# A decode block with its backward pass: a third of the score tiles shared with ScalarE, a reordered start-up, and V loads on another queue

## The chip, the cores and the metric

The kernel runs on one core of one Trainium2 chip. The metric is device time in microseconds (us) from the first to the last instruction, of single executions; I quote medians. The engines are called PE (matmul), DVE (vector), ACT (scalar), POOL (GpSimd) and SP (sync); each has its own instruction list, and in the traces here ran it as laid out (in the changed kernel the reciprocal comes 9 score tiles behind the maximum, in the list and in the trace alike).

## The reference, cut to what matters

One token passes an attention layer with 32 heads over a cache of 8192 positions, then a small MLP; the gradients of nearly all inputs are wanted too. What the change touches is the forward attention:

```python
D, Hq, Sk, Dh = 640, 32, 8192, 192
mod = (silu(c) @ w_mod)                        # 640 x 3840, six vectors of 640
h = layernorm(x) * (1 + ca) + sa
q = h @ wq                                     # 640 x 6144
scores = einsum('bhqd,bhkd->bhqk', q, k) * Dh ** -0.5
p = softmax(scores); o = einsum('bhqk,bhkd->bhqd', p, v)
x = x + ga * (o @ wo)
# ... MLP with w3, w4; then the gradients, among them dk and dv of 100 MB each
```

K and V of one head are 3.15 MB each in bf16. They are read once forward and once backward, and dK and dV are written.

## The kernel before

A head's K lies in the on-chip memory (SBUF) as 128 partitions x 64 tiles x 192. Five large buffers (`big`, tag `kv`) hold K, V and, when needed, weights. For a head DVE does 64 fused multiply-and-reduce instructions, one for each tile:

```python
    for h in range(H):
        Kt = big.tile([P, NT, Dh], BF16, tag="kv", name="Kt");  nc.sync.dma_start(out=Kt, in_=Kd[h])      # h > 0
        Vt = big.tile([P, NT, Dh], BF16, tag="kv", name="Vt");  nc.scalar.dma_start(out=Vt, in_=Vd[h])
        # ... wo for a pair of heads
        for t in range(npe, NT):
            nc.vector.tensor_tensor_reduce(out=junk_tile(Dh), in0=Kt[:, t, :], in1=qb, ...,
                                           op0=ALU.mult, op1=ALU.add, accum_out=sT[:, t:t + 1])
        nc.vector.reduce_max(out=mx, in_=sT, axis=AX.X)                # "the maximum"
        # ... PE transpose, DVE max, PE broadcast, ACT scale
        nc.scalar.activation(out=eT, in_=sT, func=ACT.Exp, bias=negb, scale=scale, accum_out=rs)
        nc.tensor.matmul(z_ps, lhsT=ones_f, rhs=rs, start=True, stop=True)
        nc.vector.reciprocal(out=rZb_all[:, h:h + 1], in_=z_ps)        # "the reciprocal"
        for t in range(NT):
            nc.tensor.matmul(o_ps, lhsT=eT_bf[:, t:t + 1], rhs=Vt[:, t, :], ...)
        nc.scalar.activation(out=o_row, in_=o_ps, func=ACT.Copy, scale=rZb_all[0:1, h:h + 1])
        # ... o_row to columns of oT, by PE and ACT
        if h % 2 == 1:
            nc.vector.tensor_copy(out=oT_bf[...], in_=oT[...])         # "the column copy"
            # ... 15 small matmuls with wo
        if h == max(0, H - 3):
            # ... load w3 on SP and w4 on ACT into two of the five large buffers
```

The program is written in dataflow; a compile-time scheduler fixes the order of every engine's list from its own model of durations, and inserts the waits.

## Time and profile before

| | before |
|---|---|
| median of 16 runs | 1883.7 us (1877.7 to 1887.1) |
| first score tile starts | 68.25 us |
| maximum of the last head | 682.80 us |
| from there to the end | 1199 us |
| DVE busy / idle between these two | 592.4 / 22.1 us |

The prediction shows the strips and windows. Two lines more from the page of before: source and destination, issuing queue, count, size, and the median us from issue to landing.

```profile
Kt<-in_A_k_cache_dram SPq DMA_DIRECT2D x32, 3072.0 KB, 13.7
Vt<-in_A_v_cache_dram ACTq DMA_DIRECT2D x32, 3072.0 KB, 14.9
```

And what DVE waited for in 100 to 600 us (total us, times, longest):

```profile
DVE ao_part L478 <- PE ao_ps L475: 5.7, 9, 0.6
DVE gm L452 <- PE mxT_ps L450: 1.1, 3, 0.7
DVE rZb_all L463 <- PE z_ps L462: 1.0, 4, 0.3
```

DVE hardly waits for anything in the steady heads.

### The profile page before, as it was taken

The numbers are of one execution on the slowest core, as the hardware profiler recorded it, in microseconds if no ns is written. First come the engines' busy times: TensorE is split into PE (matmuls) and PEld (weight loads), VectorE is DVE, ScalarE is ACT, GpSimd is POOL, SyncE is SP. The second block draws the span as 40 slices with busy tenths as digits, with TensorE's granted clock in tenths as the row PEclk, the third lists the DMA queues.
The fourth block names the chain that finished last, engine by engine and source line by source line (L and its number), as shares of the span: only waits on it lengthen the run. The fifth ranks groups of instructions, "written<-read, shape, count | busy, mean of one in ns | idle before, by whom it ended". The sixth has DMA issues, their size and how long they took to land.

```text
span 1881.7 us, 25108 instructions
## 1 busy us (share of the span) xinstructions
PE 635.7 (34%) x5307; PEld 523.1 (28%) x5307; DVE 1724.4 (92%) x11076; ACT 876.4 (47%) x2603; POOL 1.7 (0%) x12
## 2 busy tenths in 40 slices
PE   5145443554455452223232232322313223232232
PEld 3134433443344341112131221211212112121120
DVE  2599999999999767999999999999999999999987
ACT  1000000000000013767867777776776777777660
POOL 0000000000000000000000000000000000000000
PEclk9567766676667665556566565655656656565565
DMA  9778888888888741999999999999999999999995
GB/s 385 301 288 351 341 358 334 352 350 340 353 343 359 296 156 44 383 392 409 398 406 390 413 413 390 400 426 394 405 399 398 396 401 419 406 399 409 398 354 212
DMA packets 82263, 675.41 MB, mean 359 GB/s; under 512 B 4662, under 2 KB 50492, under 8 KB 57532
## 3 DMA queue, kind: packets, MB, share of 16 engines
q1 hardware_dynamic: 45656, 345.26, 46.7%
q10 hardware_dynamic: 36452, 328.54, 41.9%
q14 instruction: 114, 0.93, 0.1%
q8 instruction: 41, 0.67, 0.1%
HBM read 447.88 MB, written 225.91 MB: 358 GB/s over the span
## 4 chain that ended last, share of the span: by engine, by line
DVE 58%; DMA 23%; PE 5%; issue 1%; ACT 1%; DVEq 0%; SPq 0%; ACTq 0%
DVE junk L445 20%; DVE junk L644 20%; DMA out_dram<-dKst 13%; DMA Vt_b<-in_A_v_cache_dram 10%; DVE dKst L658 7%; DVE dVst L634 2%; PE dq_ps L668 2%; PE o_ps L466 1%; DVE junk L712 1%; DVE junk L591 1%; DMA Kt<-in_A_k_cache_dram 1%; DVE sT L445 1%; DVE junk L680 1%; DVE dpT L644 1%; PE c_ps L202 1%
## 5 line engine op out<-in xcount | busy, mean ns | idle before, releaser
L644 DVE CUSTOM_DVE_ANT_0 junk<-Vt_b,do_bcast 128x192 bf16<-128x192 bf16 x2048 | 576.0, 351 | 14.1 <-DMA Vt_b<-in_A_v_cache_dram 14.0
L445 DVE CUSTOM_DVE_ANT_0 junk<-Kt,q_bcast 128x192 bf16<-128x192 bf16 x2048 | 578.1, 345 | 8.2 <-DMA Kt<-in_A_k_cache_dram 8.1
L632 ACT ACTIVATE dVst<-do_bcast,pT 128x192 bf16<-128x192 bf16 x1536 | 541.9, 443 | 50.1 <-DVE dhAT L684 43.0
L668 PE MATMUL dq_ps<-Kt_b,dsT_bf 128*1 128x192 bf16 x2048 | 238.5, 294 | 638.2 <-ACT dsT_bf L652 616.1
L668 PEld LDWEIGHTS <-dsT_bf 128*1 128x1 bf16 x2048 | 202.7, 101 | 696.8 <-ACT dsT_bf L652 668.4
L658 DVE TENSOR_SCALAR dKst<-q_bcast,dsT 128x192 bf16<-128x192 bf16 x1376 | 249.4, 262 | 1.8 <-DVE dsT L650 0.3
L656 ACT ACTIVATE dKst<-q_bcast,dsT 128x192 bf16<-128x192 bf16 x672 | 235.5, 440 | 4.0 <-ACT dsT_bf L652 4.0
L466 PE MATMUL o_ps<-Vt,eT_all 128*1 128x192 bf16 x2048 | 227.5, 286 | 0.0
L466 PEld LDWEIGHTS <-eT_all 128*1 128x1 bf16 x2048 | 196.5, 98 | 23.8
L468 ACT ACTIVATE o_row<-o_ps,rZb_all 1x192 f32<-1x192 f32 x32 | 13.2, 412 | 405.3 <-PE o_ps L466 183.5
L644 DVE DVE_READ_ACCUMULATOR2_ANT dpT<- 128x1 f32 x2048 | 163.7, 80 | 0.0
L445 DVE DVE_READ_ACCUMULATOR2_ANT sT<- 128x1 f32 x2048 | 151.9, 74 | 0.0
L634 DVE TENSOR_SCALAR dVst<-do_bcast,pT 128x192 bf16<-128x192 bf16 x512 | 94.4, 260 | 0.0
L652 ACT CAST dsT_bf<-dsT 128x64 bf16<-128x64 f32 x32 | 7.8, 244 | 164.5 <-DVE dsT L650 164.5
L456 ACT ACTIVATE negb<-nb_ps 128x1 f32<-128x1 f32 x32 | 5.5, 171 | 156.7 <-PE nb_ps L454 155.6
L475 PE MATMUL ao_ps<-oT_bf,wof 128*128 128x1 bf16 x240 | 8.6, 165 | 136.9 <-DVE oT_bf L471 136.9
L209 PE MATMUL c2b_tp<-ident_f,doT 128*3 128x128 f32 x16 | 6.0, 374 | 122.8 <-DVE doT L591 122.8
L475 PEld LDWEIGHTS <-wof 128*128 128x128 bf16 x240 | 8.8, 104 | 136.6 <-issue 136.4
L454 PE MATMUL nb_ps<-gm,ones_f 1*128 1x1 f32 x64 | 15.7, 313 | 89.8 <-DVE gm L452 89.8
L680 DVE CUSTOM_DVE_ANT_0 junk<-wqb,dq_b 128x384 bf16<-128x384 bf16 x80 | 43.9, 549 | 0.8 <-ACT dq_b L131 0.8
L591 DVE CUSTOM_DVE_ANT_0 junk<-wob,dao_b 128x640 bf16<-128x640 bf16 x48 | 37.1, 817 | 2.8 <-DMA wob<-in_A_wo_dram 1.8
L209 PEld LDWEIGHTS c2b_tp<-ident_f,doT 128*3 128x3 f32 x16 | 1.3, 81 | 135.3 <-DVE doT L591 135.3
(220 smaller groups left out, 581.8 us busy)
## 6 DMA issues: line engine op xcount, KB each, us to landing
Kt<-in_A_k_cache_dram SPq DMA_DIRECT2D x32, 3072.0 KB, 13.7
Vt<-in_A_v_cache_dram ACTq DMA_DIRECT2D x32, 3072.0 KB, 14.9
Vt_b<-in_A_v_cache_dram SPq DMA_DIRECT2D x32, 3072.0 KB, 17.9
Kt_b<-in_A_k_cache_dram SPq DMA_DIRECT2D x32, 3072.0 KB, 15.4
out_dram<-dVst ACTq DMA_DIRECT2D x32, 3072.0 KB, 18.8
out_dram<-dKst ACTq DMA_DIRECT2D x32, 3072.0 KB, 22.4
wq_sb<-in_A_wq_dram SPq DMA_DIRECT2D x3, 2560.0 KB
wof<-in_A_wo_dram SPq DMA_DIRECT2D x16, 480.0 KB, 11.3
```

The costliest lines, as they stand in the source:

```text
L202: nc.tensor.matmul(ps, lhsT=m, rhs=prodp[:, cc:cc + 1], start=(i == 0), stop=(i == len(pieces) - 1))
L445: nc.vector.tensor_tensor_reduce(out=junk_tile(Dh), in0=Kt[:, t, :], in1=qb, scale=1.0, scalar=0.0, op0=ALU.mult, op1=ALU.add, accum_out=s ...
L466: nc.tensor.matmul(o_ps, lhsT=eT_bf[:, t:t + 1], rhs=Vt[:, t, :], start=(t == 0), stop=(t == NT - 1))
L591: nc.vector.tensor_tensor_reduce(out=junk_tile(D), in0=wob[:, k, :], in1=dao_b, scale=1.0, scalar=0.0, op0=ALU.mult, op1=ALU.add, accum_ou ...
L632: nc.scalar.activation(out=dVst[:, t, :], in_=dob, func=ACT.Copy, scale=pT[:, t:t + 1])
L634: nc.vector.tensor_scalar(out=dVst[:, t, :], in0=dob, scalar1=pT[:, t:t + 1], scalar2=None, op0=ALU.mult)
L644: nc.vector.tensor_tensor_reduce(out=junk_tile(Dh), in0=Vt[:, t, :], in1=dob, scale=1.0, scalar=0.0, op0=ALU.mult, op1=ALU.add, accum_out= ...
L656: nc.scalar.activation(out=dKst[:, t, :], in_=qb, func=ACT.Copy, scale=dsT[:, t:t + 1])
L658: nc.vector.tensor_scalar(out=dKst[:, t, :], in0=qb, scalar1=dsT[:, t:t + 1], scalar2=None, op0=ALU.mult)
L668: nc.tensor.matmul(dq_ps, lhsT=dsT_bf[:, t:t + 1], rhs=Kt[:, t, :], start=(t == 0), stop=(t == NT - 1))
L680: nc.vector.tensor_tensor_reduce(out=junk_tile(W), in0=wqb[:, j, 0:W], in1=dq_b[:, 0:W], scale=1.0, scalar=0.0, op0=ALU.mult, op1=ALU.add, ...
L712: nc.vector.tensor_tensor_reduce(out=junk_tile(WH), in0=wm_sb[:, j, q2 * WH:(q2 + 1) * WH], in1=dmod_b[:, m0 * P + q2 * WH:m0 * P + (q2 + ...
```

## The change

Its intent: give DVE less work per score tile by letting ACT, nearly idle in the forward pass, do a third of the reductions; and start the first head before all weights are there. The diff's core, cuts marked:

```diff
-        Kt0, Vt0 loads; modulation chunks 0 and 1; all three blocks of wq; modulation chunks 2 to 5
+    wmA = mod_load(0, 2 * DC)                      # all on the sync queue, in this order
+    wqA = wq_load(0, [0, WQCH])
+    # K of head 0, K of head 1, V of head 0, rest of the first wq block
+    mod_use(0, 2 * DC, wmA)                        # ... layer norm ...
+    wq_use(0, 0, WQBIG, wqA, "s")
@@ the heads
-            nc.scalar.dma_start(out=Vt, in_=Vd[h])
+            nc.gpsimd.dma_start(out=Vt, in_=Vd[h])
@@ the score tiles
+                if (t % fwd_act_den) < fwd_act_num:          # 1 of 3: 22 of 64
+                    pr = prodq.tile([P, Dh], BF16, tag="prod", name="prod")      # six buffers
+                    nc.vector.tensor_tensor(out=pr, in0=Kt[:, t, :], in1=qb, op=ALU.mult)
+                    nc.scalar.activation(out=pr, in_=pr, func=ACT.Copy, accum_out=sT[:, t:t + 1])
+                else:
                     nc.vector.tensor_tensor_reduce(...)
@@ after a head
+        if h in (5, 12):  # wq blocks 2 and 3: load and use
+        if h == 18:       # modulation columns 10 to 24: load and use
+        if h == 22:       # modulation columns 25 to 29: load and use
# ... rows of c, x, grad_out on the sync queue with three buffers; junk tiles 640 wide instead of 768
```

Three things are changed at once: the start-up with the moved loads, the split of the tiles, and the queue of V.

More of the change, by code (lines that the diff above doesn't have):

```diff
@@ L49 @@
     fwd_pe_groups: int = 0,
+    fwd_act_num: int = 1, fwd_act_den: int = 3,
     bwd_pe: bool = False,
@@ L96 @@
     junkp = ctx.enter_context(tc.tile_pool(name="junkp", bufs=3))
+    prodq = ctx.enter_context(tc.tile_pool(name="prodq", bufs=6))
     psum = ctx.enter_context(tc.tile_pool(name="psum", bufs=2, space=bass.MemoryType.PSUM))
-    JW = max(D, 6 * P, Dh, 768)
+    JW = max(D, Dh, 512)
     def junk_tile(width):
@@ L102, in junk_tile, with big_view @@
         return jt[:, 0:width]
+    def big_view(name, a, b):
+        assert a * b <= NT * Dh
+        t = big.tile([P, NT, Dh], BF16, tag="kv", name=name)
+        flat = t.rearrange("p t d -> p (t d)")
+        return flat[:, 0:a * b].rearrange("p (a b) -> p a b", b=b)
     ident_bf = const.tile([P, P], BF16, name="ident_bf")
@@ L316, in dots_via_pe @@
                 nc.tensor.matmul(out_ps[:, t:t + 1], lhsT=VB[:, tl, :], rhs=col[0:DhB, 1:2], start=False, stop=True)
-    with tc.tile_pool(name="ldrows", bufs=2) as ldrows:
-        cT = load_row_as_col(c_row_d, DC, "cT", nc.sync, ldrows)
-        xT = load_row_as_col(x_row_d, DC, "xT", nc.scalar, ldrows)
-        gT = load_row_as_col(g_row_d, DC, "gT", nc.scalar, ldrows)
+    ldrows = ctx.enter_context(tc.tile_pool(name="ldrows", bufs=3))
+    cT = load_row_as_col(c_row_d, DC, "cT", nc.sync, ldrows)
+    xT = load_row_as_col(x_row_d, DC, "xT", nc.sync, ldrows)
+    gT = load_row_as_col(g_row_d, DC, "gT", nc.sync, ldrows)
     sigT = const.tile([P, DC], FP32, name="sigT")
@@ L338, with mod_load, mod_use @@
     WQCH = 512
-    def big_view(name, a, b):
-        assert a * b <= NT * Dh
-        t = big.tile([P, NT, Dh], BF16, tag="kv", name=name)
-        flat = t.rearrange("p t d -> p (t d)")
-        return flat[:, 0:a * b].rearrange("p (a b) -> p a b", b=b)
+    def mod_load(k, k1):
+        wmt = big_view("wm_sb", DC, (k1 - k) * P)
+        nc.sync.dma_start(out=wmt, in_=wm_d[:, :, k * P:k1 * P])
+        return wmt
+    def mod_use(k, k1, wmt):
+        for m0 in range(k, k1, WMC):
+            m1 = min(k1, m0 + WMC)
+            col_times_wT_to_col(modT[:, m0:m1], wmt[:, :, (m0 - k) * P:(m1 - k) * P], scT_bf, DC, m1 - m0, "mod")
@@ new lines, with wq_load, wq_use @@
+    WQBIG = 2048
+    def wq_load(b0, cuts):
+        wq_sb = big_view("wq_sb", DC, WQBIG)
+        for c0, c1 in zip(cuts[:-1], cuts[1:]):
+            nc.sync.dma_start(out=wq_sb[:, :, c0:c1], in_=wq_d[:, :, b0 + c0:b0 + c1])
+        return wq_sb
+    def wq_use(b0, c0, c1, wq_sb, eng=None):
+        for n0 in range(c0, c1, WQCH):
+            bp = psum.tile([P, WQCH], FP32, tag="bc", name="q_bp")
+            for j in range(DC):
+                nc.tensor.matmul(bp, lhsT=hArep[:, j, :], rhs=wq_sb[:, j, n0:n0 + WQCH],
+                                 start=(j == 0), stop=(j == DC - 1))
+            evac(q_bcast[:, b0 + n0:b0 + n0 + WQCH], bp, eng)
@@ L345 @@
+    wmA = mod_load(0, 2 * DC)
+    wqA = wq_load(0, [0, WQCH])
     Kt0 = big.tile([P, NT, Dh], BF16, tag="kv", name="Kt")
     nc.sync.dma_start(out=Kt0, in_=Kd[0])
+    Kt1 = big.tile([P, NT, Dh], BF16, tag="kv", name="Kt")
+    nc.sync.dma_start(out=Kt1, in_=Kd[1])
     Vt0 = big.tile([P, NT, Dh], BF16, tag="kv", name="Vt")
-    nc.scalar.dma_start(out=Vt0, in_=Vd[0])
-    with tc.tile_pool(name="prow", bufs=2) as prow:
-        def mod_chunk(k):
-            m0, m1 = k * WMC, min(MC, (k + 1) * WMC)
-            wm_sb = prow.tile([P, DC, WMC * P], BF16, tag="wm", name="wm_sb")
-            nc.sync.dma_start(out=wm_sb[:, :, 0:(m1 - m0) * P], in_=wm_d[:, :, m0 * P:m1 * P])
-            col_times_wT_to_col(modT[:, m0:m1], wm_sb, scT_bf, DC, m1 - m0, "mod")
-        mod_chunk(0)
-        mod_chunk(1)
-        saT = modT[:, 0 * DC:1 * DC]
-        caT = modT[:, 1 * DC:2 * DC]
-        layernorm_col(xT, DC, n0T, r0, "ln0")
-        nc.vector.tensor_scalar(out=ca1, in0=caT, scalar1=1.0, scalar2=None, op0=ALU.add)
-        nc.vector.tensor_tensor(out=hAT, in0=n0T, in1=ca1, op=ALU.mult)
-        nc.vector.tensor_tensor(out=hAT, in0=hAT, in1=saT, op=ALU.add)
-        nc.vector.tensor_copy(out=hArep, in_=hAT.unsqueeze(2).to_broadcast([P, DC, P]))
-        WQBIG = (NT * Dh) // DC
-        WQBIG -= WQBIG % WQCH
-        assert WQBIG >= WQCH
-        for b0 in range(0, HD, WQBIG):
-            b1 = min(HD, b0 + WQBIG)
-            wq_sb = big_view("wq_sb", DC, WQBIG)
-            nc.sync.dma_start(out=wq_sb[:, :, 0:b1 - b0], in_=wq_d[:, :, b0:b1])
-            for n0 in range(b0, b1, WQCH):
-                n1 = min(b1, n0 + WQCH)
-                bp = psum.tile([P, WQCH], FP32, tag="bc", name="q_bp")
-                for j in range(DC):
-                    nc.tensor.matmul(bp[:, 0:n1 - n0], lhsT=hArep[:, j, :], rhs=wq_sb[:, j, n0 - b0:n1 - b0],
-                                     start=(j == 0), stop=(j == DC - 1))
-                evac(q_bcast[:, n0:n1], bp[:, 0:n1 - n0])
-        for k in range(2, (MC + WMC - 1) // WMC):
-            mod_chunk(k)
@@ new lines @@
+    nc.sync.dma_start(out=Vt0, in_=Vd[0])
+    nc.sync.dma_start(out=wqA[:, :, WQCH:WQBIG], in_=wq_d[:, :, WQCH:WQBIG])
+    mod_use(0, 2 * DC, wmA)
+    saT = modT[:, 0 * DC:1 * DC]
+    caT = modT[:, 1 * DC:2 * DC]
+    layernorm_col(xT, DC, n0T, r0, "ln0")
+    nc.vector.tensor_scalar(out=ca1, in0=caT, scalar1=1.0, scalar2=None, op0=ALU.add)
+    nc.vector.tensor_tensor(out=hAT, in0=n0T, in1=ca1, op=ALU.mult)
+    nc.vector.tensor_tensor(out=hAT, in0=hAT, in1=saT, op=ALU.add)
+    nc.vector.tensor_copy(out=hArep, in_=hAT.unsqueeze(2).to_broadcast([P, DC, P]))
@@ L422 @@
         else:
-            Kt = big.tile([P, NT, Dh], BF16, tag="kv", name="Kt")
-            nc.sync.dma_start(out=Kt, in_=Kd[h])
+            if h == 1:
+                Kt = Kt1
+            else:
+                Kt = big.tile([P, NT, Dh], BF16, tag="kv", name="Kt")
+                nc.sync.dma_start(out=Kt, in_=Kd[h])
             Vt = big.tile([P, NT, Dh], BF16, tag="kv", name="Vt")
-            nc.scalar.dma_start(out=Vt, in_=Vd[h])
+            nc.gpsimd.dma_start(out=Vt, in_=Vd[h])
         if h % 2 == 0:
@@ L444 @@
             for t in range(npe, NT):
-                nc.vector.tensor_tensor_reduce(out=junk_tile(Dh), in0=Kt[:, t, :], in1=qb, scale=1.0, scalar=0.0,
-                                               op0=ALU.mult, op1=ALU.add, accum_out=sT[:, t:t + 1])
+                if (t % fwd_act_den) < fwd_act_num:
+                    pr = prodq.tile([P, Dh], BF16, tag="prod", name="prod")
+                    nc.vector.tensor_tensor(out=pr, in0=Kt[:, t, :], in1=qb, op=ALU.mult)
+                    nc.scalar.activation(out=pr, in_=pr, func=ACT.Copy, accum_out=sT[:, t:t + 1])
+                else:
+                    nc.vector.tensor_tensor_reduce(out=junk_tile(Dh), in0=Kt[:, t, :], in1=qb, scale=1.0, scalar=0.0,
+                                                   op0=ALU.mult, op1=ALU.add, accum_out=sT[:, t:t + 1])
         mx = small.tile([P, 1], FP32, tag="mx", name="mx")
@@ L479 @@
             nc.vector.tensor_tensor(out=aoutT, in0=aoutT, in1=ao_part, op=ALU.add)
+        if h in (5, 12):
+            wqn = wq_load((1 if h == 5 else 2) * WQBIG, [0, WQBIG])
+            wq_use((1 if h == 5 else 2) * WQBIG, 0, WQBIG, wqn, "s")
+        if h == 18:
+            wmB = mod_load(2 * DC, MC - DC)
+            mod_use(2 * DC, MC - DC, wmB)
+        if h == 22:
+            wmC = mod_load(MC - DC, MC)
+            mod_use(MC - DC, MC, wmC)
         if h == max(0, H - 3):
@@ L544 @@
     dn2T = work.tile([P, DC], FP32, tag="dn2T", name="dn2T")
-    FH = F // 2
-    dn2p = work.tile([P, DC, 2], FP32, tag="dn2p", name="dn2p")
+    NQ = (F + JW - 1) // JW
+    FH = F // NQ
+    assert FH * NQ == F
+    dn2p = work.tile([P, DC, NQ], FP32, tag="dn2p", name="dn2p")
     for j in range(DC):
-        for q2 in range(2):
+        for q2 in range(NQ):
             nc.vector.tensor_tensor_reduce(out=junk_tile(FH), in0=w3_sb[:, j, q2 * FH:(q2 + 1) * FH],
```

## The prediction

> **What bounds the kernel now.** I read the strip of busy tenths first, because the kernel has stages with different limits.
>
> ```profile
> DVE  2599999999999767999999999999999999999987
> ACT  1000000000000013767867777776776777777660
> ...
> DMA  9778888888888741999999999999999999999995
> ```
>
> One column is 47 us. The vector engine (DVE) is full nearly everywhere. In the first two columns it is not: the kernel is loading. Columns 3 to 14 are the forward pass over 32 heads: DVE full, the scalar engine (ACT) almost empty, DMA at 8 tenths. From column 17 on, the backward pass, DMA is full as well. The diff touches start-up and forward pass only, so I cut the time into stages with the view of windows:
>
> ```profile
> core 0: us, PE busy (x) PEld busy (x) DVE busy (x) ACT busy (x) POOL busy (x), PEclk, DMA share, GB/s
> 68.00:683.00 615.00, 281.08 (x2488) 242.07 (x2488) 592.81 (x4244) 41.07 (x187) 0.00 (x0) 0.67 0.82 331
> 683.00:760.00 77.00, 30.18 (x277) 22.64 (x278) 42.43 (x161) 23.11 (x41) 0.00 (x0) 0.54 0.21 71
> 760.00:1830.00 1070.00, 286.12 (x2252) 235.19 (x2251) 1037.33 (x6505) 801.71 (x2350) 0.00 (x0) 0.60 0.98 400
> ```
>
> Forward: DVE 592.81 of 615 us, ACT 41 of 615, DMA at a share of 0.82 moving 331 GB/s. So DVE sets its pace, with DMA second. Backward: DMA at 0.98 and 400 GB/s; nothing in the change helps there, and I take its length as constant.
>
> Why the forward pass starts only at 68 us is told by the timeline of start-up (start, length):
>
> ```profile
> 2.74 0.25 ACTq L261 DMA_DIRECT2D gT_rb<-in_grad_out_dram  x1
> ...
> 18.50 0.48 DVE L263 CAST gT_rf<-gT_rb 1x640 f32<-1x640 bf16 x1 [7.91 <-DMA gT_rb<-in_grad_out_dram]
> ...
> 21.41 0.94 SPq L353 DMA_DIRECT2D wm_sb<-in_w_mod_dram  x2
> ...
> 67.16 0.83 PE L282 MATMUL mod_ps<-scT_bf,wm_sb 128*128 128x1 bf16 x25 [1.29 <-DMA wm_sb<-in_w_mod_dram]
> ...
> 68.25 0.36 DVE L445 CUSTOM_DVE_ANT_0 junk<-Kt,q_bcast 128x192 bf16<-128x192 bf16 x1
> ```
>
> A 1 KB row of grad_out lands behind a 3 MB load issued before it; the modulation weights are not asked for until 21 us; and the first score on DVE stands behind the last of the modulation and all three blocks of wq. DVE does nothing useful for those 68 us, while DMA is busy with loads most of which head 0 doesn't need.
>
> Then the price of one of the 64 tiles of a head, from group rows and from the spacing of starts:
>
> ```profile
> L445 DVE CUSTOM_DVE_ANT_0 junk<-Kt,q_bcast 128x192 bf16<-128x192 bf16 x2048 | 578.1, 345 | 8.2 <-DMA Kt<-in_A_k_cache_dram 8.1
> ```
> ```profile
> 311.16 0.35 DVE L445 CUSTOM_DVE_ANT_0 junk<-Kt,q_bcast 128x192 bf16<-128x192 bf16 x1
> 311.44 0.08 DVE L445 DVE_READ_ACCUMULATOR2_ANT sT<- 128x1 f32 x1
> 311.44 0.35 DVE L445 CUSTOM_DVE_ANT_0 junk<-Kt,q_bcast 128x192 bf16<-128x192 bf16 x1
> ```
> ```profile
> 1199.81 7.69 ACT L632 ACTIVATE dVst<-do_bcast,pT 128x192 bf16<-128x192 bf16 x22
> ```
>
> Mean durations overlap; the spacing is what counts. A reduce starts every 0.28 us (311.16, 311.44), so 64 cost 17.9 us of a head's 19.2 (615 / 32). ACT, in the backward pass, does 22 comparable activations in 7.69 us, 0.35 us each against a listed 443 ns.
>
> **What the skill says.** (1) "VectorE: DVE Perf Modes", section "The perf-mode tier table (the rule you actually need)": a bf16 tensor_tensor in SBUF runs at two elements a cycle and no faster, where copies and tensor_scalar reach four. This trace has no wide bf16 tensor_tensor, so it neither confirms nor denies it. It does show the reduce at one element a cycle: 128x192 takes 0.28 us of spacing, and the 128x640 one in the chain of waits 0.74, so 0.46 us for 448 more elements. (2) "ScalarE: Activation LUTs", section "What ACT_TABLE_LOAD costs": an activation with immediate scale costs 186 ns + 0.833 ns an element, each pointer operand 93 ns more, and neighbours overlap by about 93 ns. For 192 elements with one pointer scale that gives 439 ns and a spacing of 346; the trace has 443 and 350, so it agrees. (3) "SBUF — State Buffer", section "Who interferes with whom": DMAs issued from GpSimd need it to write descriptors through a port that DVE can hold in its two-port modes; tensor_tensor has none. No GpSimd DMA is in this trace. (4) "DMA: Bandwidth & Descriptors", section "Issuing engines are not separate DMA queues": another issuing queue brings no bandwidth. The page's 358 GB/s per core from memory is exceeded here, 400 in the backward window, so I use the measured rate.
>
> **The change part by part.**
>
> *22 of 64 score tiles per head are split.* Tiles 0, 3, ... 63 lose their fused reduce (0.28 us on DVE) and get a DVE multiply into a product buffer of six, then an ACT copy with accumulation. The multiply, by estimate from (1): the reduce's 0.28 us holds 192 cycles at one element a cycle, about 0.20 us; at two a cycle that is 0.10, and the 0.08 left over stays, so 0.18. The 16 single-source tensor_scalars that the chain shows in 2.87 us have the same 0.18 spacing, which tells me 0.18 is about what a small instruction costs anyway. DVE per head: 42 x 0.28 + 22 x 0.18 = 11.8 + 4.0 = 15.7 us instead of 17.9. The rest (max, reciprocal, small copies: 19.2 - 17.9 = 1.3, part of it waits) stays: 17.0 us. Saving 2.2 x 32 = 70 us if DVE stays the bound.
>
> ACT per head: 22 x (0.26 spacing without the pointer + about 0.15 for reading the accumulator; the exponential's read row lasts 186 ns) = 9.0 us, plus 1.3 us it has now (41.07 / 32). 10.3 of 17: not the bound.
>
> *DMA per head.* Two tiles of 3.146 MB and half of a 0.49 MB block of wo: 6.54 MB. At the ceiling that 331 GB/s at a share of 0.82 implies (404), 16.2 us. So DMA stands 0.8 us below the new DVE pace, and DVE cannot gain much more than this.
>
> *Start-up.* In the new order, all on the sync queue: rows, 1.64 MB of modulation weights, 0.66 MB of wq, K of head 0 (3.15 MB): 5.4 MB at 388 GB/s is 14 us, plus 2 to begin, plus sharing with V of head 1 that can start on the GpSimd queue once the modulation's buffer is free. Under it lie the row work, layer norm, 50 small matmuls and one 512-wide q block. First score at about 20 us instead of 68.25: 48 us earlier. This is not all gain.
>
> *What is moved comes back.* wq blocks 2 and 3 (2 x 2.62 MB) and the other 20 of 30 modulation columns (3.28 MB) now load in the middle of the heads 5, 12, 18 and 22: 8.5 MB, 21 us of DMA. Each also takes one of the five large buffers out of the K and V rotation, and PE, ACT or DVE may wait for it in program order. With DMA and DVE this close little of it hides: I put 5 us on each, 20 in all.
>
> *Small parts.* V issued from GpSimd: issued as soon as a buffer is free, rather than at ACT's place in its own order; worth little while DVE is the bound. Narrower junk tiles: 15 reduces of 512 instead of 10 of 768 once, under 1 us lost.
>
> *Sum.* End of the forward scores: 20 + 32 x 17.0 + 20 = 584, plus 0.7 us a head (22) for the coupling that the change adds (DVE waits for ACT's product buffers, and DMA jitter at 95% use): 606. Now it is 683. Gain 77 us, and the rest of the program unchanged: 1883 - 77 = 1806.
>
> Check by bytes: K, V, wo, wq, the modulation, w3, w4 and the first backward V are 229 MB up to the end of the forward pass; at 395 to 404 GB/s that takes 567 to 580 us. 606 respects it, and gains much above 105 us are impossible.
>
> **Rivals.** *A: DMA becomes the bound at once.* For it: 16.2 us against 17.0, five buffers for K and V, and a load of K takes a median 13.7 us to land now, with DMA at 0.82; its slack per head shrinks from 5.5 us to about 3. Against: loads land sooner when issued sooner. It would give 18 us per head: about 1830. *B: ACT blocks DVE.* ACT works in order, and in its queue the scaling of the output row waits for 64 matmuls: these lasted 5.4 to 8.0 us in the timeline, and the list of waits puts 174.8 us of ACT's forward idling on them. If accumulations stand behind such a wait, six product buffers cover only 6 x 0.73 = 4.4 us of DVE's work and DVE stops. Against: the order is laid out with those waits in mind, and ACT has 6 us of slack. Bad luck of 2 us per head gives 1865. *C: the multiply does not run at two a cycle.* Then it costs 0.28 like the reduce, DVE saves nothing per head, and only the start-up's 48 less 20 is left: about 1855. *D: better than thought.* All moved loads hide and DMA sets 16.5 us a head: 20 + 528 + 15 = 563, stopped by the bytes at about 575: 1775.
>
> **Range and chances.** The middle is 1806. A and a mild B reach 1845; D limits the other side. Range 1780 to 1845. Two per cent faster is 1845. B at its worst or C alone end above that, neither likely, since start-up alone pays 48 us before its bill. Faster 0.87, within 2% 0.11, slower 0.02: to be slower the forward pass would need more than 21 us a head.
>
> **What would show it.** First score near 20 us; the multiply spaced about 0.18 us; forward heads 17 to 18 us apart; ACT's forward busy time near 330 us; DMA share in the forward window above 0.92; backward window still about 1070 us at 400 GB/s. If the DVE waits name ACT or the product tile, B is right; if they name K with DMA at 0.98, A; a multiply at 0.28, C. I am wrong altogether if GpSimd's DMAs land much later than 15 us, or if the backward pass changes.

## The result, and the profile after

| | before | after |
|---|---|---|
| median | 1883.7 us (16 runs) | 1803.7 us (8 runs, 1796.3 to 1806.3) |
| ratio | | 0.957 (95%: 0.956 to 0.959) |
| first score tile | 68.25 | 18.13 |
| maximum of the last head | 682.80 | 600.05 |
| DVE busy / idle between | 592.4 / 22.1 | 516.3 / 65.6 |
| from there to the end | 1199 | 1198 |

Ratios are the mean time of one kernel's runs over that of the other's of the same rounds, so not quite the ratio of the medians quoted.

The whole gain lies before the last maximum, and it adds up: the start is 50.1 us earlier, DVE's work is 76.1 us less, its idle time is 43.5 us more; -50.1 - 76.1 + 43.5 = -82.7, and 600.05 - 682.80 is the same.

The strips of the changed kernel (one column is now 45 us), and its three stages by windows:

```profile
DVE  7798998989997579999999999999999999999988
ACT  4565565656664348677678678678678678678660
...
DMA  9999999898996329999999999999999999999995
```
```profile
18.00:600.00 582.00, 314.31 (x2643) 258.16 (x2643) 516.32 (x3538) 343.87 (x1607) 15.87 (x30) 0.72 0.93 383
600.00:677.00 77.00, 29.61 (x274) 21.98 (x274) 43.01 (x170) 23.45 (x42) 0.00 (x0) 0.54 0.23 83
677.00:1748.00 1071.00, 286.89 (x2255) 235.88 (x2255) 1038.33 (x6510) 801.82 (x2350) 0.00 (x0) 0.60 0.98 400
```

Columns as in the prediction. The first number behind the window is its length, then PE, PE loads, DVE, ACT, POOL busy. DVE is no longer solid in the forward pass, DMA nearly is (0.93, 383 GB/s), and the backward window is what it was: 1071 us at 400 GB/s.

The multiply and the two reduces of a group of three tiles, from the timeline (start, length):

```profile
100.38 0.25 DVE L462 TENSOR_TENSOR prod<-Kt,q_bcast 128x192 bf16<-128x192 bf16 x1
100.55 0.35 DVE L465 CUSTOM_DVE_ANT_0 junk<-Kt,q_bcast 128x192 bf16<-128x192 bf16 x1
100.83 0.08 DVE L465 DVE_READ_ACCUMULATOR2_ANT sT<- 128x1 f32 x1
100.83 0.35 DVE L465 CUSTOM_DVE_ANT_0 junk<-Kt,q_bcast 128x192 bf16<-128x192 bf16 x1
...
101.11 0.25 DVE L462 TENSOR_TENSOR prod<-Kt,q_bcast 128x192 bf16<-128x192 bf16 x1
```

The multiply takes 0.17 us of spacing (100.38 to 100.55), a reduce 0.28. ACT's share in the page's groups:

```profile
L463 ACT ACTIVATE prod<-prod 128x192 bf16<-128x192 bf16 x704 | 253.2, 360 | 164.2 <-DVE prod L462 163.6
L463 ACT ACTIVATION_READ_ACCUMULATOR prod<-prod 128x1 f32 x704 | 131.6, 187 | 0.0
```

ACT idles 164 us for products of DVE: it is the faster of the two. But what does DVE wait for, with ACT ahead? The waits of DVE in 100 to 540 us (total us, times, longest):

```profile
DVE rZb_all L483 <- PE z_ps L482: 17.8, 24, 0.8
DVE oT_bf L491 <- ACT oT L166: 12.5, 13, 1.8
DVE prod L462 <- DMA Kt<-in_A_k_cache_dram: 5.0, 2, 4.2
```

The reciprocal and the column copy, which cost about nothing before (1.3 us in all). They come in nearly every head, 0.75 us, and in every second head, about 1 us. Adding up these waits over the whole forward pass from the timeline gives 24.9 us for the reciprocal and 25.8 for the column copy. Two of them, 2.4 and 8.4 us at 554 to 565 us, fall into a stall for K that the kernel before has too (see w34_late); 39.9 us are left. In most of the steady heads the maximum of a head is followed by the maximum of the next after 16.7 us in every other head and 17.4 to 19 us in those between.

Neither instruction was touched by the diff. So I looked at the order that the compiler laid out for DVE, counting score tiles between the maximum of a head and these two (heads 8 to 10; T a multiply, r a fused reduce, the number the head whose K it reads):

```
before          between two maxima: 63 r8, 1 r9           reciprocal 61 tiles behind the maximum, column copy 62
after           21 T8, 40 r8, 1 T9, 2 r9                  reciprocal  9 tiles behind the maximum, column copy 41
```

Nine tiles are 2.2 us of DVE's time; in the timeline maximum, transpose, exponential and sum take 3.3 us. DVE arrives at the reciprocal too early and stands. Before, it came 61 tiles later and never noticed. Which part of the change moved it?

### The profile page after: what moved, and what is told of

Read it like the earlier page. It is cut to its first block, busy times and chain, and to the rows that moved or that the text cites.

```text
span 1798.2 us, 25965 instructions
## 1 busy us (share of the span) xinstructions
PE 653.1 (36%) x5307; PEld 530.6 (30%) x5307; DVE 1643.9 (91%) x10376; ACT 1176.6 (65%) x4017; POOL 18.2 (1%) x43
## 4 chain that ended last, share of the span: by engine, by line
DVE 60%; DMA 22%; PE 13%; ACT 4%; issue 1%; SPq 0%; DVEq 0%; ACTq 0%
DVE junk L675 23%; DVE junk L465 11%; DVE dKst L689 10%; DMA out_dram<-dKst 8%; DMA Vt_b<-in_A_v_cache_dram 8%; PE o_ps L486 7%; DVE prod L462 4%; DMA Kt<-in_A_k_cache_dram 3%; DVE dVst L665 3%; DMA Vt<-in_A_v_cache_dram 2%; DVE junk L622 1%; ACT dVst L663 1%; DVE junk L711 1%; DVE junk L743 1%; PE c_ps L211 1%
## 5 line engine op out<-in xcount | busy, mean ns | idle before, releaser
L465 DVE CUSTOM_DVE_ANT_0 junk<-Kt,q_bcast 128x192 bf16<-128x192 bf16 x1344 | 422.8, 348 | 0.0
L463 ACT ACTIVATE prod<-prod 128x192 bf16<-128x192 bf16 x704 | 253.2, 360 | 164.2 <-DVE prod L462 163.6
L486 PE MATMUL o_ps<-Vt,eT_all 128*1 128x192 bf16 x2048 | 237.5, 293 | 2.1 <-DMA Vt<-in_A_v_cache_dram 2.1
L486 PEld LDWEIGHTS <-eT_all 128*1 128x1 bf16 x2048 | 202.1, 101 | 30.3 <-DMA Vt<-in_A_v_cache_dram 2.2
L462 DVE TENSOR_TENSOR prod<-Kt,q_bcast 128x192 bf16<-128x192 bf16 x704 | 172.4, 248 | 8.8 <-DMA Kt<-in_A_k_cache_dram 5.7
L463 ACT ACTIVATION_READ_ACCUMULATOR prod<-prod 128x1 f32 x704 | 131.6, 187 | 0.0
L465 DVE DVE_READ_ACCUMULATOR2_ANT sT<- 128x1 f32 x1344 | 105.0, 78 | 0.0
L470 PE MATMUL mxT_ps<-ident_f,mx 128*1 128x128 f32 x32 | 11.6, 363 | 199.5 <-DVE mx L468 199.5
## 6 DMA issues: line engine op xcount, KB each, us to landing
Vt_b<-in_A_v_cache_dram SPq DMA_DIRECT2D x32, 3072.0 KB, 16.7
Vt<-in_A_v_cache_dram POOLq DMA_DIRECT2D x31, 3072.0 KB, 15.1
```

Of the source, the lines that this page charges most:

```text
L462: nc.vector.tensor_tensor(out=pr, in0=Kt[:, t, :], in1=qb, op=ALU.mult)
L463: nc.scalar.activation(out=pr, in_=pr, func=ACT.Copy, accum_out=sT[:, t:t + 1])
```

## The experiments

All in three rounds beside the kernel before, in three sets on different chips (medians of before: 1880.4, 1883.1 and 1883.7 us; each ratio is against its own set). The rows "before" and "after" are those of the result; each other row is the median of four runs. "Start" is the new start-up with the moved loads and the small rest of the diff, "split" the 22 tiles, "queue" V of heads 1 to 31 on POOL. The eight combinations:

| start | split | queue | run | us | ratio | first score | last maximum |
|---|---|---|---|---|---|---|---|
| | | | before | 1883.7 | 1 | 68.25 | 682.8 |
| x | | | start_v_act | 1839.1 | 0.977 | 18.12 | 637.4 |
| | x | | split_only | 1976.1 | 1.051 | 35.55 | 772.9 |
| | | x | queue_only | 1912.0 | 1.015 | 68.34 | 711.2 |
| x | x | | v_on_act | 1922.9 | 1.022 | 18.13 | 718.8 |
| x | | x | start_only | 1867.5 | 0.993 | 18.14 | 664.9 |
| | x | x | split_queue | 1826.3 | 0.970 | 35.75 | 627.2 |
| x | x | x | after | 1803.7 | 0.957 | 18.13 | 600.1 |

From the last maximum to the end it is 1197 to 1203 us in all eight: everything is decided before it. At a threshold of 2%, start_only and queue_only count as the same as before and v_on_act as unclear (1.020 to 1.025); but their intervals lie clear of 1 (0.991 to 0.995 and 1.014 to 1.017 for the first two). The 35.55 and 35.75 us of the two runs with the old start-up and the split are those of the first few tiles only: DVE then waits for weights, and the first maximum comes at 83.5 and 84.2 us, against 86.4 before.

### start_only: the changed kernel without the split

```diff
-    fwd_act_num: int = 1, fwd_act_den: int = 3,
+    fwd_act_num: int = 0, fwd_act_den: int = 3,
```

> The changed kernel with every score tile back on the fused DVE reduce; the new start-up, the moved loads and the GpSimd queue stay. Theory 1 (the bill of the prediction): first score at 18 us instead of 68, but 20 us of moved loads come back, so 1850 to 1860. Theory 2 (read from the changed trace: DMA has room beside a DVE-bound head, so the moved loads are nearly free): heads stay at 19.2 us, forward pass ends near 633 us, 1830 to 1838.

Measured: 1867.5 us, slower than both theories. The first score came at 18.14 us, 50 us early, yet the last maximum only 18 us early. The timeline gives DVE 28.6 us of waits for the reciprocal and 20.3 for the column copy; the laid-out order has them 7 and 35 tiles behind the maximum. So the two waits don't come from the split.

### split_only: the kernel before with the split

```diff
+                if (t % fwd_act_den) < fwd_act_num: ...   # as in the change, six product buffers
```

> The kernel before with only the split of 22 of 64 tiles. Theory 1 (the prediction's 2.2 us a head, less 0.7 for coupling): 48 us, 1835. Theory 2 (read from the changed trace, where heads are 18.2 us apart against 19.2): 32 us, 1851. Rival: without the moved loads there is no coupling at all, 70 us, 1813. First score stays at 68 us in all three.

Measured: 1976.1 us, 5% slower than before: all three figures missed, in sign too. Its waits of DVE in 100 to 600 us:

```profile
DVE junk L452 <- DMA Kt<-in_A_k_cache_dram: 126.3, 20, 7.6
```

Six us in nearly every head for K, while DMA in these 500 us had a share of only 0.70. The split by itself makes the kernel wait for data with a memory path that isn't full. (Its first score moved too, to 35.55 us, but that won only 3 us: see above.)

### v_on_act: the changed kernel with V back on ACT

```diff
-            nc.gpsimd.dma_start(out=Vt, in_=Vd[h])
+            nc.scalar.dma_start(out=Vt, in_=Vd[h])
```

> The changed kernel with the V loads of heads 1 to 31 issued from ACT again. Theory: which engine issues them brings no bandwidth, V has slack, so 1795 to 1812, within 1% of the changed kernel. Rival: ACT, now full of accumulations, issues V late, PE and DVE wait for V: over 1825.

Measured: 1922.9 us. One word turns 0.957 into 1.022. The theory fell; the rival had the direction, but not the wait: DVE waits for K, whose queue was not touched. Its longest waits in 100 to 600 us, and the timeline of one head:

```profile
DVE junk L465 <- DMA Kt<-in_A_k_cache_dram: 86.1, 16, 8.4
```
```profile
223.86 24.29 SPq L439 DMA_DIRECT2D Kt<-in_A_k_cache_dram  x2
223.86 0.36 ACT L463 ACTIVATE prod<-prod 128x192 bf16<-128x192 bf16 x1
223.87 0.35 ACTq L441 DMA_DIRECT2D Vt<-in_A_v_cache_dram  x1
...
224.27 0.41 ACT L488 ACTIVATE o_row<-o_ps,rZb_all 1x192 f32<-1x192 f32 x1
...
225.69 0.23 DVE L468 TENSOR_REDUCE mx<-sT 128x1 f32<-128x64 f32 x1
...
242.27 0.36 DVE L465 CUSTOM_DVE_ANT_0 junk<-Kt,q_bcast 128x192 bf16<-128x192 bf16 x1 [7.67 <-DMA Kt<-in_A_k_cache_dram]
```

A K is asked for at 223.86 (two such issues are merged into this line), as soon as a finished head gives its buffer back; the maximum follows; and at 242.27, when the K lands, DVE resumes after 7.67 us of nothing. Why does it need that K so early, in the middle of a head? The laid-out order:

```
v_on_act     between two maxima: 17 T9, 27 r9, 14 r10, 5 T10
split_only   between two maxima: 17 T9, 27 r9, 14 r10, 5 T10
after        between two maxima: 21 T9, 40 r9,  2 r10, 1 T10
```

With V on ACT the list of DVE runs some 20 tiles into the next head before it takes the maximum of this one. In v_on_act DVE comes to the next K 31 tiles and 8.9 us behind the maximum (225.69 to 234.6), because the first reduces of the next head are interleaved with the last multiplies of this one, while a K takes a median 17.6 us from issue to landing. With V on POOL it comes there after 61 tiles, 15 us, and the wait for the reciprocal on top.

ACT's list in v_on_act differs from that of the changed kernel in that the V load stands among ACT's accumulations:

```
Activation prod,sT <- prod          [waits DVE]     five of them shown, the last tiles of a head
DMACopy Vt <- in_A_v_cache          [waits for earlier DMAs]
Activation o_row <- o_ps, rZb       [waits PE]
Activation negb <- nb_ps            [waits PE]
Activation prod,sT <- prod          [waits DVE]     first of the next head
```

It is tempting to say that ACT stands at this load and the product buffers stay full. The trace does not show that. At 223.87 the load goes out while ACT works on without a gap; 26 of the 31 V loads go out so, four with a pause of under 1 us, one with 4.4 us; and DVE's waits for ACT's products sum to 5.3 us (another 10.2 us before the maximum). What costs the time is the order in which DVE's list was laid out. That the scheduler reckons with a standstill of ACT, and fills it with fused reduces of the next head that don't need ACT, would fit the order (some 27 reduces in a row, then multiply and reduce in turn), but it is a guess; no run shows what its model holds. The order itself, the same in both runs with split and V on ACT, and that DVE pays with waits for K, is shown. More large buffers, which could let a K be asked for earlier, were not tried.

### w34_late: w3 and w4 loaded after the last head

```diff
-        if h == max(0, H - 3):
+        if h == max(0, H - 1):
```

> The changed kernel with the loads of w3 and w4 placed after the last head instead of after head 29. Theory: in both kernels these two take two of the five large buffers, so that K of head 30 is issued only at the end of head 29 and DVE stands some 13 us; moved, this stall goes: 1788 to 1793. Rival: the two loads then land after the forward pass and the 13 us come back there: 1800 to 1806.

Measured: 1788.3 us (ratio 0.952), as the theory said. The stall is a single line in the changed kernel's chain of waits in order of time (start, length):

```profile
553.00 14.31 DMA Kt<-in_A_k_cache_dram
```

It is in the kernel before too, with 12.64 us at 632.67: w3 and w4 hold two of five buffers from head 29 on. In the changed kernel's list of waits most of this stall goes by other names (8.4 us at the column copy, 2.4 at the reciprocal), since DVE comes to those first and ends by waiting 0.8 us for K itself.

### start_v_act: start-up alone, V on ACT

start_only with V on the scalar queue as in v_on_act.

> The new start-up and moved loads alone: no split, V of heads 1 to 31 issued from ACT. Theory Q (the GpSimd queue changes the order that the compiler lays out: the reciprocal and the copy of the output columns move up to 7 and 35 tiles behind the maximum and DVE waits for them, which cost the start-only kernel some 49 us; with V on ACT they stand 56 and more tiles behind it): the 50 us of an earlier first score are seen nearly whole, 1833 to 1842. Rival M (the moved loads ate the start-up's gain): stays at 1860 to 1870.

Measured: 1839.1 us, as theory Q said. The last maximum comes 45.4 us earlier than before; of 50.1 us won at the start at most about 5 go to the moved loads. In 20 of 32 heads the reciprocal stands 51 to 65 tiles behind the maximum, not in all as I had put; it is nearer, 13 to 32, in the heads around the moved loads, and nearer too in the first head and the last three. Its waits sum to 5.6 us.

### queue_only: the kernel before with V on POOL

The edit of v_on_act the other way round, on the kernel before.

> The kernel before with V of heads 1 to 31 issued from GpSimd, nothing else. Theory Q: the same two waits of DVE appear, 35 to 50 us: 1915 to 1930. Rival: issuing from another engine changes nothing, 1878 to 1888. The prediction said: worth little.

Measured: 1912.0 us, 1.5% or some 28 us slower than before, a little under the range of theory Q. Its waits of DVE in 100 to 600 us are these two and no others:

```profile
DVE rZb_all L463 <- PE z_ps L462: 22.0, 25, 0.9
DVE oT_bf L471 <- ACT oT L157: 12.7, 13, 1.7
```

A change of a load's queue, and nothing else in the program, put two waits into an engine that neither issues nor reads that load's data.

### split_queue: split and queue on the kernel before

split_only with V on POOL.

> The kernel before with the split and the GpSimd queue, old start-up. Theory Q (the queue takes V's wait for a buffer out of ACT's order, so that the split works as in the changed kernel, heads 18 us apart): 68 + 32 x 17.8 + 12 for w3 and w4 = 650, so 1848 to 1860. Rival (the split needs the new start-up too, or the slowness of the split-only kernel is ACT's lack of time): over 1930.

Measured: 1826.3 us, 22 us better than theory Q's range. Its heads are 16.7 and 17.5 us apart in turn, where I had put 17.8; that is most of the difference. The first score came at 35.75 us and not at 68, since the order had DVE begin head 0 between the weight blocks, but DVE then waited for those, and the first maximum came at 84.2 us, under 2 us earlier than the sum had it. Against split_only the queue alone is worth 150 us.

### tail_w34: reciprocal and column copy placed later, w3 and w4 late

```diff
             for t in range(npe, NT):
+                if t == 16: <reciprocal, output row and columns of the head before>
+                if t == 60: <column copy and wo matmuls of the pair before; then load the next wo>
                 if (t % fwd_act_den) < fwd_act_num:
```

> The changed kernel with w3 and w4 loaded after the last head (1788 alone) and with the reciprocal and the column copy of a head put 16 and 60 tiles into the next head. Theory: DVE's 41 us of waits for these go; DVE then needs some 16.0 us a head, and DMA, with 16.2 and the moved loads, takes over: 1755 to 1768. Rival: the time was DMA's all along and the waits only change their name to K: 1783 to 1792.

Measured: 1773.2 us (1770.2 to 1774.0), ratio 0.941: the fastest kernel, correct, 1.7% under the changed one (0.941 / 0.957). It came 5 us above the theory's range. Against w34_late the two moves are worth some 15 to 19 us (1788.3 to 1773.2, or 0.952 to 0.941 by the ratios of the two sets), less than the about 40 us of waits that they take away. The waits for the reciprocal and the copy are gone from the list (the reciprocal now stands 13 tiles behind the maximum, the copy 57), K has come in, and the window says why:

```profile
DVE prod L470 <- DMA Kt<-in_A_k_cache_dram: 17.2, 9, 5.1
DVE modT L293 <- PE mod_ps L291: 4.9, 3, 2.0
```
```profile
18.00:568.00 550.00, 314.11 (x2636) 257.91 (x2639) 513.26 (x3538) 328.62 (x1605) 15.84 (x30) 0.73 0.97 402
```

The first is 100 to 540 us, the second the whole forward pass: DMA at a share of 0.97 and 402 GB/s. Undisturbed heads are 15.8 us apart, less than the 16.2 us that their bytes need by the prediction's estimate, so the next K comes late now and then.

### tail_w34_half: the same with 32 of 64 tiles split

```diff
-    fwd_act_num: int = 1, fwd_act_den: int = 3,
+    fwd_act_num: int = 1, fwd_act_den: int = 2,
```

> The fastest kernel so far (late w3 and w4, later reciprocal and column copy: 1773) with 32 of 64 tiles split instead of 22. DVE's work falls by 10 x 0.11 = 1.1 us a head, 35 us. Theory: DMA is the bound there already (402 GB/s at a share of 0.97 in the forward pass), so 1765 to 1776. Rival: DVE still sets the pace in the heads that are 15.8 us apart: 1740 to 1755.

Measured: 1776.6 us, no faster than tail_w34. DVE's work in the forward pass fell from 513 to 485 us and none of it was gained:

```profile
18.00:570.00 552.00, 315.11 (x2640) 257.96 (x2643) 484.96 (x3218) 434.43 (x2245) 15.82 (x30) 0.73 0.98 405
```

With DMA at 0.98 and 405 GB/s, the likeliest limit of this forward pass is DMA. ACT, with ten more tiles a head, has come into DVE's waits as well: 11.4 and 7.1 us in 100 to 540 us, beside 23.2 for K. More relief for DVE is worth nothing here.

### v_on_sp: V on the sync queue

```diff
-            nc.gpsimd.dma_start(out=Vt, in_=Vd[h])
+            nc.sync.dma_start(out=Vt, in_=Vd[h])
```

> The changed kernel with V of heads 1 to 31 issued from the sync engine instead of GpSimd. Laid out, no tile of the next head stands before the maximum, but the reciprocal stands directly behind it (9 tiles in the changed kernel) and the column copy 25 tiles behind (41). Theory (the position in DVE's order decides, not the kind of queue): DVE waits about 3.1 us a head for the reciprocal instead of 0.8 and some 1.7 us more a pair for the copy, about 100 us in all, 1895 to 1915. Rival (taking V out of ACT is all that counts): 1798 to 1815.

Measured: 1925.5 us, above the theory's range and far from the rival: out of ACT is not enough. In 100 to 600 us DVE waits

```profile
DVE rZb_all L483 <- PE z_ps L482: 45.8, 23, 2.0
DVE oT_bf L491 <- ACT oT L166: 35.4, 11, 9.6
DVE modT L293 <- PE mod_ps L291: 15.2, 4, 7.5
```

The wait for the reciprocal is 2.0 us a head, less than the 3.1 I put (the links ahead of it, the maximum and its transpose, take the rest: 11.9 and 10.7 us of waits more), that for the copy larger. DMA's share was 0.76 over the forward pass. K and V now share one list as well; how much of the time is that, and how much the order of DVE, this run doesn't tell.

### no_mid_loads: the moved loads taken away

```diff
-        if h in (5, 12): ...    if h == 18: ...    if h == 22: ...
+    # once, behind the first block: q_bcast blocks 2 and 3, modT columns 10 to 29 copied from the first ones
```

> The changed kernel without the four moved loads; their values are filled with copies of the first ones, so the result is wrong on purpose. Prediction: they cost 20 us, so 1782 to 1786. Rival, from the runs with the start-up alone, where they took at most 5 us: 1797 to 1801. Between, at 1788 to 1794, if DMA near its ceiling lets half through.

Measured: 1788.0 us, with a wrong result. The moved loads cost 16 us in the changed kernel (1803.7 - 1788.0), between the prediction's 20 and the at most 5 seen in start_v_act. DMA's share in the forward pass is 0.93 in the changed kernel and 0.89 in start_v_act; that this is the reason isn't tested.

### prod2: two product buffers instead of six

```diff
-    prodq = ctx.enter_context(tc.tile_pool(name="prodq", bufs=6))
+    prodq = ctx.enter_context(tc.tile_pool(name="prodq", bufs=2))
```

> The changed kernel with two product buffers instead of six; the laid-out order of DVE is the same. The prediction's rival B says the buffers are what covers ACT's waits for the 64 matmuls: with two they cover 1.5 us, DVE stops at each exponential and each output row, 1 to 2 us a head: 1835 to 1870. Rival (ACT's waits are short in this order: 43 us in the whole forward pass): 1804 to 1815.

Measured: 1805.7 us, 2 us more than with six. In the order of the changed kernel ACT's waits are too short to stop DVE for long: 5.2 us of waits of DVE's multiplies for ACT in all.

## Why the prediction was right, and which step was wrong

The time was forecast at 1806 and measured at 1803.7, and faster by over 2% had the odds. The steps:

- **Bound.** Right: DVE sets the forward pass, the backward pass didn't move (1071 us, 400 GB/s).
- **Start-up.** First score at 20 us forecast, 18.1 measured; 48 us forecast, 50.1 measured.
- **Multiply at two elements a cycle.** 0.18 us forecast, 0.17 measured; 70 us less work forecast, 76.1 measured. Rival C is out.
- **ACT.** About 330 us busy forecast, 343.9 measured; the share of DMA above 0.92 forecast, 0.93 measured.
- **Moved loads.** 20 us forecast, 16 measured in no_mid_loads.
- **Coupling.** 22 us forecast, for ACT's product buffers and DMA jitter. DVE's idle time grew by 43.5 us, of which no_mid_loads takes away 15.5 (idle 50.1 against 65.6); 28 remain. The size was close; the reason was not. Product buffers play next to no part (prod2), and the waits that grew are those of two instructions that the compiler's order moved forward: from 1.3 us to 39.9, outside the stall for w3 and w4, while smaller waits shrank.
- **Rival A** (DMA the bound at once) was not the state of the changed kernel, but its next one: tail_w34 and tail_w34_half are there. Its figure in the prediction, about 1830, isn't what its 18 us a head give by the prediction's own sum: 20 + 576 + 20 = 616 us, so 1816, or 1838 with the 22 us of coupling.
- **The step that failed** is the one among the "Small parts": "V issued from GpSimd: issued as soon as a buffer is free, rather than at ACT's place in its own order; worth little while DVE is the bound." Alone it costs 28 us (queue_only), and with start and split it is worth 119 us (1922.9 against 1803.7), half as much again as the whole net gain. Without it the split loses: 1976 against 1883.7, 1922.9 against 1839.1. The prediction treated the split as a saving by itself, at 2.2 us a head; in both runs with V on ACT it is a loss, and with V on the sync queue too the kernel is slow (1925.5). Rival B was the nearest: it named ACT's list as the danger, but looked at ACT blocking DVE, and trusted that "the order is laid out with those waits in mind". In v_on_act DVE waits 15.5 us for ACT's products but 127 us for K: the order itself is what costs, by DVE's early need of K.

So a sum with right terms came out right because the diff happened to hold both halves of a pair, the split and the queue; the prediction didn't know that they were a pair, and would have called the split alone a gain. That the new queue also pulls reciprocal and column copy forward costs some 28 to 30 us where DVE has no split to gain from (queue_only against before, start_only against start_v_act). In the changed kernel later places for the two win back some 15 to 19 us (tail_w34 against w34_late); part of the rest comes back as waits for K (5.7 us in w34_late, 17.2 in tail_w34).

What stays open: why the scheduler, given V on POOL, places the reciprocal 9 tiles behind the maximum and not later. In queue_only the chip needed up to 0.9 us more for the chain than DVE was given, which fits a model of durations that is a little too fast; no run tests it. Likewise why it interleaves two heads when V is on ACT. And v_on_sp's extra time isn't split into its two causes.

## What to carry to other kernels

Before giving work to an engine that also issues loads, try those loads on other engines, and measure each: here the same split lost with V on ACT, won with V on POOL, and the changed kernel was slow with V on SP. Where a compiler fixes the order, a change of queue can reorder engines that never touch the data; compare the laid-out orders as well as the times, and look for short waits that come once a head. Run the parts of a bundle singly: here two of three parts lose alone, and together they win.

## What the Trainium skill lacked or had wrong

- "DMA: Bandwidth & Descriptors", section "Issuing engines are not separate DMA queues": initiating DMAs on several engines "will only save the time on the sequencer it takes to initiate the DMA". For bandwidth nothing here speaks against it: GB/s over DMA's share in the forward pass gives 409, 412 and 418 with V on ACT, POOL and SP. For time it is not the whole story where a compiler lays out the order: the same V loads gave 1922.9, 1803.7 and 1925.5 us. No page that I found says that the choice of the issuing engine can change the laid-out order of others.
- The same page's 358 GB/s a core, which the prediction calls exceeded, is not wrong: the page gives it for both cores of a pair streaming, and higher figures for one alone. With one core running, 402 and 405 GB/s over 550 us (tail_w34, tail_w34_half) agree with that.
- "ScalarE: Activation LUTs", section "What ACT_TABLE_LOAD costs": 186 ns + 0.833 ns an element for immediate scale gives 346 ns for 192 elements, and the trace has 360. The section has no price for the accumulator output: each accumulation here brings a separate read of 187 ns.
- "VectorE: DVE Perf Modes", section "The perf-mode tier table (the rule you actually need)": two elements a cycle for the bf16 multiply agrees (0.17 us of spacing where the fused reduce at one a cycle takes 0.28); the fused multiply-and-reduce isn't in the table.
- "SBUF — State Buffer", section "Who interferes with whom": no starved GpSimd DMA is to be seen (31 V loads, a median of 15.1 us from issue to landing); the DVE work of the forward pass is nearly all multiplies and fused reduces (704 and 1344 of them), so no run here tests the warning about two-port modes.
